# The value products of two attention pieces issued together, added up in one PSUM bank; x taken out by one ScalarE instruction a piece

## The chip, the cores and the metric

The kernel runs on one core of one Trainium2 chip. Its time is device microseconds from start to end of one execution. Each version is timed in several runs, and the median counts. The engines are named as in the profile: PE is TensorE's products, PEld its weight loads, DVE is VectorE, ACT is ScalarE, POOL is GpSimd, SP is the queue that issues nearly all transfers.

## The reference

Two layers follow each other: a local attention with a summary of the far keys, and a mixture of four experts over its output.

```python
B, H, S, D = 4, 8, 768, 64                 # attention
k_sum = k.reshape(B, H, 24, 32, D).max(axis=3)
v_sum = v.reshape(B, H, 24, 32, D).mean(axis=3)
scores_l = where(|i - j| < 16, q @ k.T / 8, -1e9)
scores_s = q @ k_sum.T / 8 + log(32)
a = softmax(concatenate([scores_l, scores_s], -1))   # sum + 1e-9
x = (a @ concatenate([v, v_sum], 2)) -> [3072, 512]

p = domain_probs / domain_probs.sum(-1)    # experts: E = 4, 512 -> 1024 -> 512
out = sum over e of p[:, e] * (relu(x @ w1[e]) @ w2[e])
```

All arrays are float32.

## The kernel before

**Pieces.** Attention is cut into 64 pieces: 4 batches, 8 blocks of 96 queries, and 2 groups of 4 heads. Piece n belongs to batch n // 16 and to group g = n % 2, so pieces n - 1 and n with n odd are the two groups of the same 96 queries. A query block needs only a window of 128 keys, and 24 summaries. Pieces 0 to 7 are made by a function of their own at the start (`first_tokens`), pieces 8 to 63 by the steps below.

**Steps of a piece.** `load_piece` fetches keys, queries and values; `stage_a` splits keys, queries and values into parts of fewer bits (the values into three bfloat16 parts, `v12` holding two and `v3` the third); `scores` forms the scores in PSUM (`psc`), takes row maxima on VectorE (`ms`, `nb`) and exponentials on ScalarE; `probs` divides by the row sum and writes the weights as float16 in `aw`: 4 heads of high parts, 4 of low parts, 4 of summaries. `transposed` turns `aw` around with one transposing transfer into `awT`. `values` multiplies: for each head, the three value parts with the weights' high part, two of them with the low part also, and the summaries `vs`. `to_x` turns what stands in PSUM into x.

**Buffers around the change.** `aw` is one of two fixed tiles: `aw1` for odd pieces below 28, `aw0` for all others, so from piece 28 on only `aw0` is used. `awT` has two buffers of its own; odd pieces below 28 take theirs from the pool of x instead. `v12` and `v3` have three buffers. PSUM has 4 banks for the experts (`ps_mm`), 2 for scores (`ps_sc`) and 2 in `ps_av`, which `px` shares with one product of the expert stage (`phd`) and with the summaries of values (`pvs`).

**Products before.** A piece has one bank, `px`. It is read as two pairs of heads (c), two columns groups (w = 0 for the products with high weights, w = 1 for those with low weights) and 96 queries. The two heads of a pair write to the lower and the upper 64 partitions, so two products with 64 weight columns each stand beside each other on the array. A product with both parts of the weights is one instruction of 192 columns; the third value part and the summaries are instructions of 96 columns. `to_x` adds the two column groups: ScalarE scales w = 1 into `xs`, VectorE adds w = 0. For pieces 8 to 15 (token block 1) ScalarE then rounds `xs` to `xh` and GpSimd subtracts to get `xl`, the two parts in which x enters the experts. From piece 16 on, `xs` is written to memory (`xd`) and read again (`xr`) when a pair of token blocks is made ready in `x_operands`.

**Order.** Token blocks of 384 rows (`TB`) are the unit of the experts: block 0, then 1, then both with the other experts, then three pairs of blocks with a seven-product scheme (`pair_units`). The expert work comes in units of a few products, and `advance` issues the attention steps between them: each step has a due time in units of pieces, and a list `ENDS` says at which due time each stage of expert work ends. From the end of the first tokens on, the instructions aren't pinned: a scheduler that replays the program on a model of the engines takes, on each engine, the ready instruction that comes first in the program, and so may put other products between the products of one piece. Transfers nearly all go through SP's queue, in the order that this scheduler gave.

The steps' due times:

```python
(k + 0.4, probs, n),
(k + 0.8, transposed, n),
(k + (1.5 if n < 2 * per else 2.0), values, n),
(k + (1.8 if n < 2 * per else 2.3), to_x, n),
```

Nearly every instruction is issued through the class `Engine`, so the profile gives all of them the line of its helper (L75). They are told apart by the names of their tiles.

Of the kernel before, what the change touches and what calls it, by code (L numbers as in the profile page):

```python
# [8 lines left out]
F32 = mybir.dt.float32  # L9
F32R = mybir.dt.float32r  # L10
BF16 = mybir.dt.bfloat16
F16 = mybir.dt.float16
AF = mybir.ActivationFunctionType
ALU = mybir.AluOpType
AX = mybir.AxisListType

P = 128
B, H, S, D = 4, 8, 768, 64
# [3 lines left out]
QB = 96  # L22
KW = 128
KA = KW + NB
NQ = S // QB
G = 4
# [4 lines left out]
NST = 5 * NB  # L31
# [14 lines left out]
ASC = 32768.0  # L46
# [16 lines left out]
def attn_moe(ctx: ExitStack, tc: tile.TileContext, qvL, qv0, v0L, kD, kT, vT, w1L, w2L, dpL, cst, out):  # L63
# [18 lines left out]
    V, A, PL, PE = (Engine(e, "rest") for e in (nc.vector, nc.scalar, nc.gpsimd, nc.tensor))  # L82
    SP = Engine(nc.sync, "load")

    def pool(name, bufs=1, **kw):
        return ctx.enter_context(tc.tile_pool(name=name, bufs=bufs, **kw))
# [3 lines left out]
    def spare_x(n):  # L90

        return n % 2 == 1 and n < XFREE

    sb = pool("sb")
    ps_mm = pool("ps_mm", 4, space=bass.MemoryType.PSUM)
    ps_sc = pool("ps_sc", 2, space=bass.MemoryType.PSUM)
    ps_av = pool("ps_av", 2, space=bass.MemoryType.PSUM)
# [21 lines left out]
    per = 2 * (TB // QB)  # L119
# [16 lines left out]
    xT = {}  # L136
    xraw = {}
    written = {}
    st = {}
# [79 lines left out]
    def stage_a(n):  # L219
        b, i, g = n // 16, (n // 2) % NQ, n % 2  # L220
        h0 = g * G
        t = st[n]
        qr = t["qv"][:, 0 : G * QB].rearrange("p (h s) -> p h s", s=QB)
        vr = t["qv"][:, G * QB :].rearrange("p (h d) -> p h d", d=D)
        kr = t["kr"]
        PL.tensor_copy(kr[:, :, KW:KA], ksum[b][:, h0 : h0 + G, :])
        ks = []
        tag, bufs = ("x", NX) if spare_x(n) else ("kl", 2)
        for half in range(2):
            k2 = sb.tile([P, 2, 2, KA], F32R, name=f"ks{n}_{half}", tag=tag, bufs=bufs)  # L230
            hs = slice(2 * half, 2 * half + 2)
            A.copy(k2[:, :, 0, :], kr[:, hs, :])
            PL.tensor_tensor(k2[:, :, 1, :], kr[:, hs, :], k2[:, :, 0, :].bitcast(F32), op=ALU.subtract)
            ks += [k2[:, 0], k2[:, 1]]
        qs = sb.tile([P, G, QB], F32R, name=f"qs{n}", tag="qs", bufs=1)
        A.copy(qs, qr)
        PL.tensor_tensor(qs[D:P], qr[D:P], qs[D:P].bitcast(F32), op=ALU.subtract)
        v12 = sb.tile([P, G, 2, D], BF16, name=f"v12_{n}", tag="v12", bufs=3)
        v3 = sb.tile([P, G, D], BF16, name=f"v3_{n}", tag="v3", bufs=3)
        A.copy(v12[:, :, 0, :], vr)  # L240
        PL.tensor_tensor(vr, vr, v12[:, :, 0, :], op=ALU.subtract)
        A.copy(v12[:, :, 1, :], vr)
        PL.tensor_tensor(v3, vr, v12[:, :, 1, :], op=ALU.subtract)
        t.update(ks=ks, qs=qs, v=(v12, v3))

    def scores(n, half):
        i = (n // 2) % NQ
        t = st[n]
        mask = masks[0 if i == 0 else (2 if i == NQ - 1 else 1)]
        if half == 0:  # L250
            t["ms"] = sb.tile([QB, G, KA], F32, name=f"ms{n}", tag="ms", bufs=2)
            t["nb"] = sb.tile([QB, G], F32, name=f"nb{n}", tag="nb", bufs=2)

            t["rs"] = sb.tile([QB, G, 2], F32, name=f"rs{n}", tag="rs", bufs=3)[:, :, 0]
        ms, nb, rs, qs, ks = (t[w] for w in ("ms", "nb", "rs", "qs", "ks"))
        heads = (2 * half, 2 * half + 1)

        def maximum(j, o, add):

            V.tensor_tensor_reduce(  # L260
                ms[:, j, :], o, add, scale=-SCALE, scalar=3.0e38,
                op0=ALU.add, op1=ALU.min, accum_out=nb[:, j : j + 1],
            )

        psc = ps_sc.tile([P, 2, 256], F32, name=f"psc{n}_{half}", tag="sc")
        for j in heads:
            o = psc[:QB, j % 2, :KA]
            PE.matmul(o, qs[:, j, :], ks[j][:, 0, :], start=True, stop=False)
            PE.matmul(o, qs[:, j, :], ks[j][:, 1, :], start=False, stop=True)
        for j in heads:  # L270
            maximum(j, psc[:QB, j % 2, :KA], mask)
        for j in heads:
            A.activation(
                ms[:, j, :], ms[:, j, :], AF.Exp, bias=nb[:, j : j + 1], scale=-1.0,
                accum_out=rs[:, j : j + 1],
            )
# [25 lines left out]
    def values(n):  # L302
        b, g = n // 16, n % 2
        t = st[n]
        awT, (v12, v3), vs = t["awT"], t["v"], vsum[b]
        px = ps_av.tile([P, 512], F32, name=f"px{n}", tag="av")
        pxv = px[:, 0 : 4 * QB].rearrange("p (c w q) -> p c w q", w=2, q=QB)
        for c in range(2):
            terms = []
            for j in (2 * c, 2 * c + 1):  # L310
                both, hi, su = awT[:, j : 2 * G : G, :], awT[:, j, :], awT[:NST, 2 * G + j, :]
                terms.append(
                    [
                        (slice(0, 2), v12[:, j, 0, :], both),
                        (slice(0, 2), v12[:, j, 1, :], both),
                        (0, v3[:, j, :], hi),
                        (0, vs[:, g * G + j, :], su),
                    ]
                )
            last = len(terms[0]) - 1  # L320
            for m in range(last + 1):
                for o in range(2):
                    w, *operands = terms[o][m]
                    PE.matmul(
                        pxv[o * D : (o + 1) * D, c, w, :], *operands, start=m == 0, stop=m == last
                    )
        t["px"] = pxv

    def x_half(name):
        return sb.tile([P, 2, TB], F32R, name=name, tag="x", bufs=NX)  # L330
# [1 line left out]
    def x_block(tb):  # L332
        return [[x_half(f"x{w}{tb}_{g}") for w in "hl"] for g in range(2)]

    def to_x(n):
        i, g = (n // 2) % NQ, n % 2
        tb, ib = n // per, i % (TB // QB)
        pxv = st.pop(n)["px"]
        xs = sb.tile([P, 2, QB], F32, name=f"xs{n}", tag="xt", bufs=2)
        A.mul(xs, pxv[:, :, 1, :], 1.0 / ASC)  # L340
        V.scalar_tensor_tensor(xs, pxv[:, :, 0, :], 1.0 / ASC, xs, op0=ALU.mult, op1=ALU.add)
        if tb < 2:
            if tb not in xT:
                xT[tb] = x_block(tb)
            xh, xl = (x[:, :, ib * QB : (ib + 1) * QB] for x in xT[tb][g])
            A.copy(xh, xs)
            PL.tensor_tensor(xl, xs, xh.bitcast(F32), op=ALU.subtract)
            return
        if (tb // 2, ib) not in xraw:
            xraw[tb // 2, ib] = dram.tile([P, 4, 2, QB], F32, name=f"xd{tb // 2}_{ib}")  # L350
        SP.dma_start(xraw[tb // 2, ib][:, 2 * g + tb % 2], xs)
        written[tb // 2, ib] = written.get((tb // 2, ib), 0) + 1

# [551 lines left out]
    steps = []  # L907
    for n in range(per, NTB * per):
        k = n + SHIFT * (n >= 2 * per)
        if n > per + 1:  # L910
            steps.append((k - 2.0, load_piece, n))
        steps += [
            (k - 0.6, stage_a, n),
            (k + 0.0, lambda m: scores(m, 0), n),
            (k + 0.3, lambda m: scores(m, 1), n),
            (k + 0.4, probs, n),
            (k + 0.8, transposed, n),
            (k + (1.5 if n < 2 * per else 2.0), values, n),
            (k + (1.8 if n < 2 * per else 2.3), to_x, n),
        ]  # L920
    for b in range(1, B):
        k = 2 * per * b + SHIFT
        steps += [(k - 2.0, setup_k, b), (k - (0.5 if b == 1 else 1.0), setup_v, b)]
# [22 lines left out]
    for (tbs, experts), end in zip(plan, ENDS):  # L946
        pair = tbs if isinstance(tbs, int) else None
        n = 2 if pair else len(tbs)
# [5 lines left out]
        parts, u, done = None, 0.0, 0.0  # L954
# [80 lines left out]
```

## Time and profile before

| | |
|---|---|
| median of 3 runs | 1190.65 us (1186.84 to 1193.61) |
| profiled execution | 1190.1 us, span 1188.3 us |
| TensorE products | 1155.9 us busy, 97% of the span |
| weight loads | 1018.8 us |
| VectorE, ScalarE, GpSimd | 640.2, 544.3, 473.2 us |
| granted TensorE clock | 0.994 |
| pieces' products (`px`) | 78.3 to 898.0 us, 896 instructions |
| memory read and written | 174.22 MB and 57.15 MB |

The span is from the first to the last instruction; the execution's time has 1.8 us more around it. Busy times of an engine count each moment once, though TensorE's products overlap: a product's length in a row is longer than the step from its start to the next one's start. What a product costs is read from the starts. After 898 us only expert work is left.

### The profile page before, as it was taken

To read this page: it belongs to the slowest core of one execution; us is meant where nothing else is said; L and a number is where in the kernel's file an instruction comes from. 1 tells how busy PE (TensorE), PEld (TensorE's weight loads), DVE (VectorE), ACT (ScalarE), POOL (GpSimd) and SP (SyncE) were. 2 spreads that over 40 slices of the span, in tenths; PEclk is the share of its full clock that TensorE was granted. 3 is DMA by queue.
4 is the path that set the end of the run, shared out by engine and by line. 5 is a ranking of instruction groups with operands and counts; after the bars stand their busy time and mean duration, and the time that the engine had idled before them with its cause. 6 is when DMAs were issued, how large, how long until landed. Compare 5 with 4: busy or idle time off the path is not lost.

```text
span 1188.3 us, 19862 instructions
## 1 busy us (share of the span) xinstructions
PE 1155.9 (97%) x6740; PEld 1018.8 (86%) x6740; DVE 640.2 (54%) x1567; ACT 544.3 (46%) x1594; POOL 473.2 (40%) x586
## 2 busy tenths in 40 slices
PE   9898899999998999999999999999999999999998
PEld 7788778888977989888898988989898998989896
DVE  6668585554797756648587543535345322323131
ACT  5577567664665746547375443535333220202020
POOL 2388686855696746546384222222203000000000
PEclk9989999999999999999999999999999999999999
DMA  6699869975986879879973758769471556556421
GB/s 238 220 283 262 241 173 270 264 198 148 319 239 193 271 236 263 245 247 289 297 240 109 211 167 268 223 195 305 115 229 42 160 176 194 179 181 201 159 98 54
DMA packets 202709, 249.60 MB, mean 210 GB/s; under 512 B 83056, under 2 KB 118896, under 8 KB 202608
## 3 DMA queue, kind: packets, MB, share of 16 engines
q1 hardware_dynamic: 202608, 248.34, 69.5%
q8 instruction: 53, 0.87, 0.3%
q14 instruction: 48, 0.39, 0.1%
HBM read 174.22 MB, written 57.15 MB: 195 GB/s over the span
## 4 chain that ended last, share of the span: by engine, by line
PE 67%; DVE 5%; DMA 2%; POOL 1%; ACT 1%; issue 1%; SPq 0%; DVEq 0%; POOLq 0%; ACTq 0%
PE po L75 37%; PE phb L75 11%; PE pha L75 7%; PE phc L75 4%; PE phd L75 4%; PE psc L75 2%; PE px L75 2%; POOL wr L75 1%; DVE xr L75 1%; DVE w1s L75 1%; DMA wr<-in_w2L 1%; PE ph L75 1%; DVE xl_t L75 1%; DVE ms L75 0%; DVE hl L75 0%
## 5 line engine op out<-in xcount | busy, mean ns | idle before, releaser
L75 PE MATMUL po<-w,hh 128*128 128x512 f32 x1536 | 482.0, 395 | 1.8 <-DVE hl L75 1.8
L75 PEld LDWEIGHTS po<-w,hh 128*128 128x128 f32 x1536 | 284.8, 189 | 63.6 <-DVE hl L75 2.3
L75 PE MATMUL po<-w,hl 128*128 128x512 f32 x768 | 303.2, 397 | 0.2 <-DVE hl L75 0.2
L75 PEld LDWEIGHTS po<-w,hl 128*128 128x128 f32 x768 | 144.7, 188 | 31.9 <-DVE hl L75 0.6
L75 POOL TENSOR_TENSOR ks<-kr,ks 128x304 fp32r<-128x304 f32 x112 | 102.1, 919 | 93.0 <-ACT ks L75 82.5
L75 PE MATMUL phb<-xh_t,w1s 128*128 128x384 f32 x384 | 114.8, 339 | 1.7 <-DVE phc L75 0.8
L75 DVE CUSTOM_DVE_ANT_0 ms<-psc,c_sb 96x152 f32<-96x152 f32 x256 | 69.0, 306 | 85.1 <-PE psc L75 82.2
L75 ACT ACTIVATE ms<-ms,nb 96x152 f32<-96x152 f32 x256 | 104.3, 415 | 19.5 <-DVE nb L75 18.6
L75 PE MATMUL pha<-xh,w 128*128 128x384 f32 x384 | 110.6, 335 | 0.0
L75 DVE SCALAR_TENSOR_TENSOR acc<-po,pw,acc 128x512 f32<-128x512 f32 x72 | 52.2, 747 | 103.9 <-PE po L75 103.9
L75 POOL TENSOR_TENSOR qv<-qv,v 128x256 f32<-128x256 f32 x56 | 42.1, 753 | 161.3 <-ACT v L75 140.0
L75 PE MATMUL ph<-xh,wh 128*128 128x384 f32 x256 | 87.7, 349 | 12.8 <-ACT wh L75 5.3
L75 PE MATMUL ph<-xh,wl 128*128 128x384 f32 x256 | 87.0, 341 | 0.4 <-POOL wl L75 0.3
L75 PE MATMUL ph<-xl,wh 128*128 128x384 f32 x256 | 86.9, 340 | 0.0
L75 ACT CAST v<-qv 128x256 bf16<-128x256 f32 x112 | 44.7, 401 | 87.5 <-PE px L75 73.4
L75 ACT CAST aw<-ms 96x512 f16<-96x512 f32 x112 | 53.4, 524 | 68.2 <-issue 49.1
L75 POOL TENSOR_TENSOR wl<-wr,wh 128x512 fp32r<-128x512 f32 x44 | 60.8, 1386 | 53.2 <-ACT wh L75 50.2
L75 DVE TENSOR_TENSOR aw<-ms,aw 96x512 f16<-96x512 f32 x112 | 71.5, 671 | 16.7 <-ACT aw L75 16.6
L75 PEld LDWEIGHTS phb<-xh_t,w1s 128*128 128x128 f32 x384 | 70.8, 188 | 4.1 <-DVE phc L75 1.7
L75 PEld LDWEIGHTS pha<-xh,w 128*128 128x128 f32 x384 | 70.5, 188 | 0.4
L75 ACT CAST ks<-kr 128x304 fp32r<-128x304 f32 x112 | 48.2, 444 | 40.3 <-PE psc L75 38.0
L75 PE MATMUL phb<-xl_t,w1s 128*128 128x384 f32 x192 | 64.3, 335 | 0.0
(123 smaller groups left out, 2190.2 us busy)
## 6 DMA issues: line engine op xcount, KB each, us to landing
w<-wd SPq DMA_DIRECT2D x80, 512.0 KB, 4.4
w1s<-wds SPq DMA_DIRECT2D x112, 256.0 KB, 3.5
w<-wd SPq DMA_DIRECT2D x84, 256.0 KB, 3.4
wr<-in_w1L SPq DMA_DIRECT2D x76, 256.0 KB, 4.3
qv<-in_qvL SPq DMA_DIRECT2D x56, 320.0 KB, 3.9
wd<-w SPq DMA_DIRECT2D x32, 512.0 KB, 4.0
wds<-w1s SPq DMA_DIRECT2D x64, 256.0 KB, 2.4
kr<-in_kD SPq DMA_DIRECT2D x56, 256.0 KB, 3.7
```

Of the source, the lines that this page charges most:

```text
L75: ins = getattr(self.engine, name)(*a, **kw)
```

## The change

`values` for an even and the odd piece after it are issued together, at the due time of the odd one (`both_values`). The two pieces share one bank, the even piece in columns 0 to 191, the odd one in 192 to 383. Each product has 96 columns, and all six of a head are added up at the same place: the column group for the low weights is gone. So a piece has 24 products of 96 columns in place of 8 of 192 and 8 of 96.

`to_x` runs once a pair. For token block 1 ScalarE scales each piece's bank half straight into `xh`, and VectorE makes `xl` from the bank and `xh`. For later pieces ScalarE scales each half into one staging tile, which holds both pieces and has one buffer (before: two of half the size), and one transfer writes it to memory. `v12` and `v3` have four buffers.

```diff
-        v12 = sb.tile([P, G, 2, D], BF16, name=f"v12_{n}", tag="v12", bufs=3)
-        v3 = sb.tile([P, G, D], BF16, name=f"v3_{n}", tag="v3", bufs=3)
+        v12 = sb.tile([P, G, 2, D], BF16, name=f"v12_{n}", tag="v12", bufs=4)
+        v3 = sb.tile([P, G, D], BF16, name=f"v3_{n}", tag="v3", bufs=4)
...
-        px = ps_av.tile([P, 512], F32, name=f"px{n}", tag="av")
-        pxv = px[:, 0 : 4 * QB].rearrange("p (c w q) -> p c w q", w=2, q=QB)
+        if g == 0:
+            t["bank"] = ps_av.tile([P, 512], F32, name=f"px{n}", tag="av")
+        else:
+            t["bank"] = st[n - 1]["bank"]
+        px = t["px"] = t["bank"][:, g * 2 * QB : (g + 1) * 2 * QB].rearrange("p (c q) -> p c q", q=QB)
...
-                both, hi, su = awT[:, j : 2 * G : G, :], awT[:, j, :], awT[:NST, 2 * G + j, :]
+                hi, lo, su = awT[:, j, :], awT[:, G + j, :], awT[:NST, 2 * G + j, :]
                 terms.append(
-                        (slice(0, 2), v12[:, j, 0, :], both),
-                        (slice(0, 2), v12[:, j, 1, :], both),
-                        (0, v3[:, j, :], hi),
-                        (0, vs[:, g * G + j, :], su),
+                        (v12[:, j, 0, :], hi),
+                        (v12[:, j, 0, :], lo),
+                        (v12[:, j, 1, :], hi),
+                        (v12[:, j, 1, :], lo),
+                        (v3[:, j, :], hi),
+                        (vs[:, g * G + j, :], su),
                 )
-            for m in range(last + 1):
+            for m in range(6):
                 for o in range(2):
-                    w, *operands = terms[o][m]
-                    PE.matmul(
-                        pxv[o * D : (o + 1) * D, c, w, :], *operands, start=m == 0, stop=m == last
-                    )
+                    PE.matmul(px[o * D : (o + 1) * D, c, :], *terms[o][m], start=m == 0, stop=m == 5)
+
+    def both_values(n):
+        values(n - 1)
+        values(n)
...
     def to_x(n):
-        pxv = st.pop(n)["px"]
-        xs = sb.tile([P, 2, QB], F32, name=f"xs{n}", tag="xt", bufs=2)
-        A.mul(xs, pxv[:, :, 1, :], 1.0 / ASC)
-        V.scalar_tensor_tensor(xs, pxv[:, :, 0, :], 1.0 / ASC, xs, op0=ALU.mult, op1=ALU.add)
+        pair = [st.pop(m)["px"] for m in (n - 1, n)]
         if tb < 2:
...
-            A.copy(xh, xs)
-            PL.tensor_tensor(xl, xs, xh.bitcast(F32), op=ALU.subtract)
+            for g in range(2):
+                A.mul(parts[g][0], pair[g], 1.0 / ASC)
+            for g in range(2):
+                V.scalar_tensor_tensor(
+                    parts[g][1], pair[g], 1.0 / ASC, parts[g][0].bitcast(F32), op0=ALU.mult, op1=ALU.subtract
+                )
             return
+        xs = sb.tile([P, 2, 2, QB], F32, name=f"xs{n}", tag="xt")
+        A.mul(xs[:, 0], pair[0], 1.0 / ASC)
+        A.mul(xs[:, 1], pair[1], 1.0 / ASC)
...
-        SP.dma_start(xraw[tb // 2, ib][:, 2 * g + tb % 2], xs)
-        written[tb // 2, ib] = written.get((tb // 2, ib), 0) + 1
+        SP.dma_start(xraw[tb // 2, ib][:, tb % 2 : 4 : 2], xs)
+        written[tb // 2, ib] = written.get((tb // 2, ib), 0) + 2
...
-            (k + (1.5 if n < 2 * per else 2.0), values, n),
-            (k + (1.8 if n < 2 * per else 2.3), to_x, n),
+        if n % 2:
+            steps += [
+                (k + (1.5 if n < 2 * per else 2.0), both_values, n),
+                (k + (1.8 if n < 2 * per else 2.3), to_x, n),
+            ]
```

More of the change, by code (lines that the diff above doesn't have):

```diff
@@ L310, in values @@
             for j in (2 * c, 2 * c + 1):
-                both, hi, su = awT[:, j : 2 * G : G, :], awT[:, j, :], awT[:NST, 2 * G + j, :]
+                hi, lo, su = awT[:, j, :], awT[:, G + j, :], awT[:NST, 2 * G + j, :]
                 terms.append(
-                    [
-                        (slice(0, 2), v12[:, j, 0, :], both),
-                        (slice(0, 2), v12[:, j, 1, :], both),
-                        (0, v3[:, j, :], hi),
-                        (0, vs[:, g * G + j, :], su),
-                    ]
-                )
-            last = len(terms[0]) - 1
-            for m in range(last + 1):
+                    (
+                        (v12[:, j, 0, :], hi),
[5 more added lines that the diff above has]
+                    )
+                )
+            for m in range(6):
                 for o in range(2):
-                    w, *operands = terms[o][m]
-                    PE.matmul(
-                        pxv[o * D : (o + 1) * D, c, w, :], *operands, start=m == 0, stop=m == last
-                    )
-        t["px"] = pxv
+                    PE.matmul(px[o * D : (o + 1) * D, c, :], *terms[o][m], start=m == 0, stop=m == 5)
+    def both_values(n):
+        values(n - 1)
+        values(n)
     def x_half(name):
@@ L335, in to_x @@
     def to_x(n):
-        i, g = (n // 2) % NQ, n % 2
+        i = (n // 2) % NQ
         tb, ib = n // per, i % (TB // QB)
-        pxv = st.pop(n)["px"]
-        xs = sb.tile([P, 2, QB], F32, name=f"xs{n}", tag="xt", bufs=2)
-        A.mul(xs, pxv[:, :, 1, :], 1.0 / ASC)
-        V.scalar_tensor_tensor(xs, pxv[:, :, 0, :], 1.0 / ASC, xs, op0=ALU.mult, op1=ALU.add)
+        pair = [st.pop(m)["px"] for m in (n - 1, n)]
         if tb < 2:
@@ L344, in to_x @@
                 xT[tb] = x_block(tb)
-            xh, xl = (x[:, :, ib * QB : (ib + 1) * QB] for x in xT[tb][g])
-            A.copy(xh, xs)
-            PL.tensor_tensor(xl, xs, xh.bitcast(F32), op=ALU.subtract)
+            parts = [[x[:, :, ib * QB : (ib + 1) * QB] for x in xT[tb][g]] for g in range(2)]
+            for g in range(2):
[3 more added lines that the diff above has]
+                    parts[g][1], pair[g], 1.0 / ASC, parts[g][0].bitcast(F32), op0=ALU.mult, op1=ALU.subtract
+                )
             return
+        xs = sb.tile([P, 2, 2, QB], F32, name=f"xs{n}", tag="xt")
+        A.mul(xs[:, 0], pair[0], 1.0 / ASC)
+        A.mul(xs[:, 1], pair[1], 1.0 / ASC)
         if (tb // 2, ib) not in xraw:
             xraw[tb // 2, ib] = dram.tile([P, 4, 2, QB], F32, name=f"xd{tb // 2}_{ib}")
-        SP.dma_start(xraw[tb // 2, ib][:, 2 * g + tb % 2], xs)
-        written[tb // 2, ib] = written.get((tb // 2, ib), 0) + 1
+        SP.dma_start(xraw[tb // 2, ib][:, tb % 2 : 4 : 2], xs)
+        written[tb // 2, ib] = written.get((tb // 2, ib), 0) + 2
     XS = ("11", "21", "22", "t1", "t2", "t3", "t4")
```

## The prediction

> **What bounds the kernel now.** I read the page's shares first, then the busy time by stretch, then TensorE's own groups, its waits, and its timeline around the changed products. The first two say whether anything off TensorE can matter.
>
> ```profile
> span 1188.3 us, 19862 instructions
> PE 1155.9 (97%) x6740; PEld 1018.8 (86%) x6740; DVE 640.2 (54%) x1567; ACT 544.3 (46%) x1594; POOL 473.2 (40%) x586
> 78.00:172.00 94.00, 83.38 (x563) 72.98 (x561) 72.35 (x172) 65.25 (x197) 74.45 (x79) 0.96 0.83 229
> 290.00:460.00 170.00, 163.61 (x1006) 143.68 (x1005) 124.70 (x282) 98.74 (x306) 115.65 (x140) 1.00 0.84 254
> 460.00:610.00 150.00, 149.02 (x864) 132.11 (x864) 99.39 (x228) 80.84 (x247) 86.42 (x108) 1.00 0.88 272
> ```
>
> Columns of the stretches: length, then busy time of PE, PEld, DVE, ACT, POOL, then clock, DMA share, GB/s. From 460 us on TensorE hardly rests (149.0 of 150 us, and so it goes on to the last products at 898), so only a change of TensorE's own work moves the end there; VectorE and ScalarE have 20 us and more to spare in each stretch. Idle TensorE time worth naming lies in 78 to 172 (10.6 us) and 290 to 460 (6.4 us). So I price TensorE's work first and the waits second.
>
> **TensorE: the products.** The groups of the value products now:
>
> ```profile
> L75 PE MATMUL px<-awT,v 128*64 128x192 f16 x448 | 36.1, 254 | 8.0 <-DMA awT<-aw 8.0
> L75 PE MATMUL px<-awT,vs 120*64 120x96 f16 x224 | 24.7, 210 | 0.0
> L75 PE MATMUL px<-awT,v 128*64 128x96 f16 x224 | 24.2, 208 | 0.0
> ```
>
> A piece has 16 of them (896 / 56): 8 of 192 columns and 8 of 96. After the change it has 24 of 96. Columns: 8 x 192 + 8 x 96 = 2304 before, 24 x 96 = 2304 after, so streaming is unchanged and only what each product and each block costs beside it counts. Busy sums don't show this, since products overlap; starts do. TensorE's timeline, one piece alone and two pieces that happen to stand together (first number the start, second the length):
>
> ```profile
> 77.78 0.40 PE L75 MATMUL po<-w,hl 128*128 128x512 f32 x1
> 78.01 0.39 PE L75 MATMUL po<-w,hh 128*128 128x512 f32 x1
> 78.33 0.40 PE L75 MATMUL px<-awT,v 128*64 128x192 f16 x6
> 78.56 0.21 PE L75 MATMUL px<-awT,vs 120*64 120x96 f16 x2
> 78.61 0.37 PE L75 MATMUL px<-awT,v 128*64 128x192 f16 x6
> 78.82 0.21 PE L75 MATMUL px<-awT,vs 120*64 120x96 f16 x2
> 78.96 0.91 PE L75 MATMUL psc<-ks,qs 128*96 128x152 f32 x8
> 79.70 0.43 PE L75 MATMUL po<-w,hh 128*128 128x512 f32 x1
> ...
> 93.46 0.33 PE L75 MATMUL ph<-xh,wl 128*128 128x384 f32 x1
> 93.64 0.34 PE L75 MATMUL ph<-xh,wh 128*128 128x384 f32 x1
> 93.91 0.40 PE L75 MATMUL px<-awT,v 128*64 128x192 f16 x6
> ...
> 94.39 0.21 PE L75 MATMUL px<-awT,vs 120*64 120x96 f16 x2
> 94.44 0.37 PE L75 MATMUL px<-awT,v 128*64 128x192 f16 x6
> ...
> 95.78 0.38 PE L75 MATMUL ph<-xl,wh 128*128 128x384 f32 x1
> ...
> 897.28 0.34 PE L75 MATMUL phd<-xh_t,w1s 128*128 128x384 f32 x1
> 897.54 0.40 PE L75 MATMUL px<-awT,v 128*64 128x192 f16 x6
> ...
> 898.17 0.73 PE L75 MATMUL po<-w,hh 128*128 128x512 f32 x2
> 898.74 0.40 PE L75 MATMUL po<-w,hl 128*128 128x512 f32 x1
> ```
>
> Inside a block the second half-piece runs from 78.61 to 78.82 plus 0.04 to 0.05 for its last pair (78.56 to 78.61): 0.25 us per half-piece, 0.50 per piece. Those 0.04 to 0.05 us are the step of one pair of 96 columns (the two products of a pair run beside each other on two halves of the array's columns), twice in a row here. Twelve such pairs make 12 x 0.043 = 0.52 us: the new form costs 0.02 us more per piece, 56 x 0.02 = **+1.1 us**.
>
> What surrounds a block is larger. The last block, one whole piece, takes 1.46 us from 897.28 to 898.74. Taken off: the phd product before it (0.18, as 93.46 to 93.64), two po products after it (0.23 each, as 77.78 to 78.01) and the piece's 0.50. That leaves 0.32 us, spread over a late first product (0.26 after its neighbour instead of 0.18), a late exit and a slow first product behind it. Is it paid by the piece or by the block? Both early blocks are followed by the same eight score products. From the last product ahead to the first behind these the single piece takes 1.69 us (78.01 to 79.70), 1.46 without its po; the two pieces take 2.14 (93.64 to 95.78), 1.96 without their ph. The second piece adds 0.50, its streaming alone. At the seam (94.39 to 94.44) nothing is lost. So the toll of about 0.3 us is paid once a block, not once a piece: that is what issuing two pieces together can save. [...]
>
> Blocks now, counted in TensorE's timeline from the first (78.33) to the last (897.54): 68. Forty-two hold one whole piece, one holds two, and 25 are fragments, because the order puts other products between the halves of some pieces. After, 28 pairs give at least 28 blocks. I don't expect 28: 12 pieces in 56 are cut now, and a pair is twice as long, so I take 12 cuts again, 40 blocks. Saved: 28 x 0.31 = **-8.7 us** (0.31, a little under the 0.32, as some of it is the slow start of what follows in any case). With no cut it is 40 x 0.31 = -12.4; with every pair cut once 12 x 0.31 = -3.7. Nearly all blocks lie where TensorE is busy without a break, so the saving is on the path.
>
> **The other engines.** What goes and what stays:
>
> ```profile
> L75 ACT ACTIVATE xs<-px 128x192 f32<-128x192 f32 x56 | 18.3, 327 | 8.4 <-PE px L75 8.4
> L75 DVE SCALAR_TENSOR_TENSOR xs<-px,xs 128x192 f32<-128x192 f32 x56 | 19.6, 349 | 8.7 <-ACT xs L75 8.5
> L75 ACT CAST xh<-xs 128x192 fp32r<-128x192 f32 x8 | 2.8, 346 | 5.6 <-DVE xs L75 5.6
> L75 POOL TENSOR_TENSOR xl<-xs,xh 128x192 fp32r<-128x192 f32 x8 | 5.6, 696 | 2.0 <-ACT xh L75 2.0
> ```
>
> The ScalarE instruction stays, 56 at 0.327. VectorE keeps 8 of 56 and loses 48 x 0.349 = 16.8 us; ScalarE loses 8 x 0.346 = 2.8 and its 5.6 us of standing behind VectorE; GpSimd loses 5.6. SP issues 24 writes to memory in place of 48, of twice the size. All of it is hidden by TensorE (VectorE is busy 124.7 of 170 us at its fullest), so I count **0**; were VectorE the bound, 16.8 us would be its worth, and that is the far end. The single staging tile is read by its write (24 of them between 172 and 898 us, one in 30 us) long before it is needed. The bank of a pair is held once instead of twice; the other user, the phd products, keeps the second one. The value tiles get a fourth buffer, and an even piece's tile still comes free by the products of the odd piece three before it, as now.
>
> **Waits.** TensorE's own, and the place at the start of the second token block (132 to 142 us):
>
> ```profile
> PE px L75 <- DMA awT<-aw: 8.0, 6, 2.6
> 132.12 0.40 PE L75 MATMUL px<-awT,v 128*64 128x192 f16 x6 [0.38 <-DMA awT<-aw]
> 137.04 1.33 PE L75 MATMUL ph<-xh,wh 128*128 128x384 f32 x4 [4.22 <-ACT xh L75]
> 136.26 0.35 DVE L75 SCALAR_TENSOR_TENSOR xs<-px,xs 128x192 f32<-128x192 f32 x1
> 138.45 0.61 PE L75 MATMUL px<-awT,v 128*64 128x192 f16 x6
> ```
>
> Piece 14's products ran at 132.12, its x waited behind VectorE until 136.26, and piece 15's products ran at 138.45. After the change both run when piece 15's transposed weights are there, so the first ph product moves from 137.04 to about 139.9 (138.45 + 1.05 of products + 0.33 of ScalarE): up to 2.9 us lost. Against it, the way from bank to x loses a VectorE step (0.35), a copy (0.35) and a GpSimd step (0.7) and ScalarE stands 5.6 us less, so piece 15 is earlier by 1 to 3 us. I take 0, with -3 and +3 as ends. The other waits for awT fall on one piece of two instead of on each; half of 8.0 is 4.0 gained if the even pieces' waits simply go, but the next paragraph takes about that back: 0.
>
> From piece 28 on all transposed weights share two buffers, and all untransposed ones a single tile:
>
> ```profile
> 310.72 2.30 SPq L75 DMA_TRANSPOSE awT<-aw  x1
> 327.06 0.40 PE L75 MATMUL px<-awT,v 128*64 128x192 f16 x6
> awT<-aw SPq DMA_TRANSPOSE x56, 4.3
> ```
>
> Piece 30 was transposed at 310.72, before piece 29's products (327.06). After, pieces 28 and 29 hold both buffers until their pair runs, so the transpose of each even piece from 30 on waits for TensorE, 17 of 36 pieces. Behind it wait the next piece's weights (the one tile is still being read) and, if the order on SP puts it ahead of a load, that load. A pair's loop is then two landings (8.6) and the making of the odd piece's weights between them, about 5 us, and 1 us of products: 15 us. By the starts of the blocks in TensorE's timeline, pairs come every 30 to 40 us after 390 us, so it is covered; between 327 and 387 us seven pieces (29 to 35) came in 60 us, 17 us a pair, so it has next to no slack there.
>
> **The sum.** -8.7 + 1.1 + 0 + 0 = -7.6 us on the profiled execution's 1190.1 (span 1188.3 and 1.8 around it): 1182.5. The median of the runs, 1190.65, stands 0.5 us above that execution, so I keep 1182.5 for both.
>
> **Rivals.** *The block is cut apart* (the change doesn't do what it says): the scheduler still fills gaps with single halves, 56 blocks: -3.7 + 1.1, 1187.5. For it: 25 fragments today; against: 42 whole pieces. *No cuts and a better start*: -12.4 + 1.1 - 3, 1176. *Weight loads set the pace.* Twelve pairs of 96 columns need a fresh set of weights each time, and 192 columns no longer cover every second load. A row with short products and heavy weights:
>
> ```profile
> 18.78 0.82 PE L75 MATMUL pav<-vf,pT 128*96 128x65 f32 x8
> 19.43 0.50 PE L75 MATMUL pT<-c_sb,ms 96*128 96x96 f32 x4
> ```
>
> Eight products of 65 columns behind 96 weight columns take 0.65 us, 0.081 each, more than their columns need. Scaled to 64 weight columns it is 0.054 a pair, 0.65 a piece instead of 0.50: 56 x 0.15 = +8.4, no gain left: 1190. Against it: two pairs in a row already step by 0.04 to 0.05. [...] *Slower: the transposes.* In that stretch, each of the four pairs leaves TensorE standing for one landing more: 4 x 4.3 = 17.2, and 1182.5 + 17 = 1199.5. It decides once the waits for awT grow by some 14 us over today's 8.0. For it: 2.6 us waits stand there already; against: TensorE has expert products to put in their place, and they are ready.
>
> **How the numbers follow.** Forecast (30 to 45 blocks, 1179 to 1186) 0.46; no cuts 0.12; cut apart 0.15; weight loads 0.09; transposes 0.18. The range reaches from below the no-cut case, 1173, to between weight loads and transposes, 1196. A change of 0.5%, 6 us, is about what can be told from none: faster is below 1184.7: 0.38 of the forecast's 0.46, 0.12 and 0.02 of the cut case, 0.52; slower above 1196.6, 0.15; within, 0.33.
>
> **What would show it.** Right: 24 products of 96 columns a piece stepping 0.042 a pair; 30 to 45 blocks; the toll still 0.3 a block; waits for awT at 5 to 11 us; VectorE near 623 us. Wrong: a step of 0.054; over 55 blocks; TensorE waits over 40 us in all, above all between 327 and 390 us or at 137 us; SP's issue of weights standing behind a transpose.

## The result, and the profile after

The changed kernel takes 1177.6 us (1174.58 to 1180.83, 6 runs) against 1189.68 in the same comparison: ratio 0.9899, 95% interval 0.9874 to 0.9924. That is 12 us faster, inside the range of the prediction (1173 to 1196) and 5 us below its 1182.5. Its profiled execution has a span of 1174.7 us, 13.5 less than before. But the steps of the forecast did not add up as forecast: the term that was to carry the gain came out at a quarter of its size, and most of the gain came from a term that had been put at zero. Ratios, here and below, leave out executions at a far lower granted clock, of which e12 had one (1603 us at 0.65).

The page's first lines, and the same stretches as before:

```profile
span 1174.7 us, 20612 instructions
PE 1150.5 (98%) x7188; PEld 1021.0 (87%) x7188; DVE 631.4 (54%) x1519; ACT 541.2 (46%) x1586; POOL 468.5 (40%) x578
78.00:172.00 94.00, 86.89 (x646) 76.58 (x645) 77.01 (x186) 65.24 (x202) 74.31 (x77) 0.98 0.92 263
290.00:460.00 170.00, 163.13 (x1105) 146.25 (x1105) 118.12 (x271) 100.92 (x311) 114.65 (x142) 0.98 0.83 252
460.00:610.00 150.00, 149.94 (x967) 133.81 (x966) 100.17 (x230) 82.58 (x254) 85.89 (x109) 1.00 0.85 268
```

Between 78 and 172 us TensorE is busy 86.9 us instead of 83.4, and the granted clock there is 0.98 instead of 0.96. From 290 to 460 nothing is better.

The value products, by group and in TensorE's timeline, one pair of pieces that was not cut:

```profile
L75 PE MATMUL px<-awT,v 128*64 128x96 f16 x1120 | 39.0, 209 | 9.4 <-DMA awT<-aw 9.4
L75 PE MATMUL px<-awT,vs 120*64 120x96 f16 x224 | 25.8, 211 | 0.1
...
199.45 0.40 PE L75 MATMUL po<-w,hl 128*128 128x512 f32 x1
199.78 0.40 PE L75 MATMUL px<-awT,v 128*64 128x96 f16 x10
200.01 0.21 PE L75 MATMUL px<-awT,vs 120*64 120x96 f16 x2
200.06 0.38 PE L75 MATMUL px<-awT,v 128*64 128x96 f16 x10
200.27 0.21 PE L75 MATMUL px<-awT,vs 120*64 120x96 f16 x2
200.32 0.38 PE L75 MATMUL px<-awT,v 128*64 128x96 f16 x10
200.53 0.21 PE L75 MATMUL px<-awT,vs 120*64 120x96 f16 x2
200.58 0.38 PE L75 MATMUL px<-awT,v 128*64 128x96 f16 x10
200.79 0.21 PE L75 MATMUL px<-awT,vs 120*64 120x96 f16 x2
200.93 0.57 PE L75 MATMUL psc<-ks,qs 128*96 128x152 f32 x4
```

From 200.06 to 200.32 six pairs of 96 columns take 0.26 us, 0.043 a pair, as priced; the seam between the two pieces (200.27 to 200.32) costs nothing. So the products are as forecast and a block still has one toll.

TensorE's largest waits, before (beside the 8.0 us for awT, shown above) and then after:

```profile
PE ph L75 <- ACT wh L75: 5.3, 4, 2.1
PE ph L75 <- ACT xh L75: 4.2, 1, 4.2
PE ph L75 <- DVE hl L75: 3.3, 4, 1.3
PE po L75 <- DVE hl L75: 1.9, 3, 1.5
```

```profile
PE px L75 <- DMA awT<-aw: 9.4, 4, 5.6
PE ph L75 <- ACT wh L75: 3.7, 2, 2.3
PE ph L75 <- DVE xl L75: 2.3, 1, 2.3
PE ph L75 <- DVE hl L75: 1.2, 1, 1.2
```

The one wait for x of block 1 fell from 4.2 to 2.3 us. The waits for `hl` (the low part of the experts' first result, made by VectorE) fell by more, from 5.2 to 1.2, and those for expert weights (`wh`) from 5.3 to 3.7.

Where the 13.5 us went, worked out from the starts in TensorE's timeline. *Edges* are the steps inside and beside blocks of value products less the usual step of each product (0.229 for po, 0.173 for 384 columns, 0.085 for scores, 0.020 for each 96 columns of a value product); *waits* are TensorE's idle times over 0.15 us, but for the 1.2 us at the very start; *slow steps* are what products away from blocks lost where each took over 0.1 us more than its usual step. In brackets is the part of the slow steps that lies in stretches of half clock; the rest came late at full clock, most of it beside a wait. The last column is when SP issued the transpose of piece 15, the last of token block 1.

| kernel | blocks | edges | waits | slow steps (at half clock) | span | piece 15 |
|---|---|---|---|---|---|---|
| before | 68 | 23.6 | 27.3 | 9.5 (4.7) | 1188.3 | 135.0 |
| changed | 57 | 21.7 | 19.1 | 5.9 (4.3) | 1174.7 | 126.4 |
| e1 fourth buffer | 66 | 23.9 | 20.9 | 10.0 (6.4) | 1184.3 | 136.1 |
| e2 sum only | 71 | 24.4 | 22.8 | 11.0 (6.8) | 1186.3 | 132.7 |
| e3 sum and buffer | 69 | 24.4 | 15.7 | 9.1 (4.7) | 1179.9 | 129.7 |
| e4 pairs and buffer | 62 | 22.4 | 23.5 | 12.6 (8.0) | 1186.6 | 131.1 |
| e5 whole blocks | 40 | 16.2 | 22.7 | 11.3 (6.6) | 1178.3 | 128.2 |
| e6 many blocks | 82 | 30.8 | 24.6 | 11.3 (7.5) | 1195.2 | 135.2 |
| e7 neutral, changed | 55 | 20.9 | 19.2 | 11.3 (7.6) | 1179.6 | 130.1 |
| e8 neutral, before | 68 | 23.9 | 24.5 | 9.9 (5.7) | 1186.7 | 136.2 |
| e9 long way in block 1 | 59 | 23.3 | 24.3 | 9.3 (7.6) | 1187.7 | 135.7 |
| e10 VectorE step back | 56 | 21.4 | 21.9 | 9.0 (5.5) | 1179.9 | 128.6 |
| e11 later in the stretch | 58 | 21.9 | 16.9 | 6.8 (3.8) | 1173.5 | 127.1 |
| e12 whole and later | 40 | 15.3 | 21.4 | 9.5 (4.6) | 1174.1 | 128.4 |

Before to changed: edges -1.9, waits -8.2, slow steps -3.6, together -13.7 of 13.5. Of the slow steps' 3.6 us only 0.4 is half clock (4.7 against 4.3).

And it happened early. At the first value product the changed trace is already 3.2 us ahead (75.1 us against 78.3), before any of the new products has run: up to there TensorE waited 2.6 us less, and between 50 and 66 us it had 3.4 us of half clock where the trace before has 6.8. This lead is not shown to come from the change: the trace of e4, which gains nothing, has it too (75.2), and that of e10, which gains 6 us, does not (78.7). The 145th po product starts at 160.8 us before and at 153.8 after (7.0 earlier), the 217th at 204.0 and 193.4 (10.6), and from there to the end the distance stays between 8.5 and 15.4.

SP's transposes, first and last of token block 1, before and then after:

```profile
68.64 2.18 SPq L75 DMA_TRANSPOSE awT<-aw  x1
...
135.00 1.33 SPq L75 DMA_TRANSPOSE awT<-aw  x1
```

```profile
66.35 1.90 SPq L75 DMA_TRANSPOSE awT<-aw  x1
...
126.44 1.31 SPq L75 DMA_TRANSPOSE awT<-aw  x1
```

Eight pieces took 66.4 us before and 60.1 after: attention itself is faster in that stretch. On TensorE none of these eight pieces stands beside its partner, though they are issued in pairs: each is a block by itself or, for piece 8, two. It is the stretch in which experts on block 0 must not run dry before x of block 1 is there.

The start of the experts on block 1, after (137.04 with a wait of 4.22 before):

```profile
129.82 0.40 PE L75 MATMUL px<-awT,v 128*64 128x96 f16 x10 [1.14 <-DMA awT<-aw]
130.46 0.74 PE L75 MATMUL psc<-ks,qs 128*96 128x152 f32 x6
131.04 0.90 PE L75 MATMUL ph<-xh,wh 128*128 128x384 f32 x4
134.24 0.44 PE L75 MATMUL ph<-xl,wh 128*128 128x384 f32 x1 [2.30 <-DVE xl L75]
```

The first ph product starts 1.2 us after piece 15's products start. It does not wait for VectorE any more; the second does, since xl is now VectorE's, behind other work in its queue (a reduction of `vch` from 132.02, row maxima from 132.89; `xl` starts at 133.83).

The slow stretch around 350 us, after:

```profile
343.69 0.40 PE L75 MATMUL px<-awT,v 128*64 128x96 f16 x10
...
349.95 0.61 PE L75 MATMUL px<-awT,v 128*64 128x96 f16 x10 [5.55 <-DMA awT<-aw]
345.00 2.82 SPq L75 DMA_TRANSPOSE awT<-aw  x1
347.00:350.00 3.00, 0.05 (x3) 0.05 (x4) 2.18 (x7) 0.92 (x4) 1.72 (x3) 0.51 0.78 125
350.00:354.00 4.00, 4.00 (x34) 3.46 (x34) 2.36 (x5) 3.04 (x10) 1.82 (x4) 0.52 0.96 286
```

Pieces 32 and 33 were issued together; 32 had its weights, 33 was transposed at 345.00, and TensorE stood 5.55 us between the two. This is the rival of the transposes, real but small: waits for awT rose from 8.0 to 9.4 us in all. The granted clock is 0.51 at the end of the wait and 0.52 in the 4 us after it.

### The profile page after: what moved, and what is told of

It is laid out like the page before. It is cut to its first block, busy times and chain, and to the rows that moved or that the text cites. A ratio compares the mean times of both kernels' runs of the same rounds, so it can differ in the third digit from the quotient of the medians.

```text
span 1174.7 us, 20612 instructions
## 1 busy us (share of the span) xinstructions
PE 1150.5 (98%) x7188; PEld 1021.0 (87%) x7188; DVE 631.4 (54%) x1519; ACT 541.2 (46%) x1586; POOL 468.5 (40%) x578
## 4 chain that ended last, share of the span: by engine, by line
PE 85%; DMA 4%; DVE 4%; POOL 3%; ACT 2%; issue 1%; SPq 1%; POOLq 0%; DVEq 0%; ACTq 0%
PE po L75 42%; PE phb L75 13%; PE pha L75 9%; PE ph L75 5%; PE phd L75 4%; PE phc L75 4%; PE psc L75 4%; PE px L75 3%; DMA vch<-in_vT 1%; PE pav L75 1%; DMA wr<-in_w2L 1%; DMA kch<-in_kT 1%; DVE ms L75 1%; SPq L75 1%; ACT ms L75 1%
## 5 line engine op out<-in xcount | busy, mean ns | idle before, releaser
L75 POOL TENSOR_TENSOR ks<-kr,ks 128x304 fp32r<-128x304 f32 x112 | 99.7, 897 | 176.8 <-ACT ks L75 160.5
L75 DVE TENSOR_TENSOR aw<-ms,aw 96x512 f16<-96x512 f32 x112 | 77.2, 723 | 21.5 <-ACT aw L75 21.3
```

The lines of the kernel that those rows point to most:

```text
L75: ins = getattr(self.engine, name)(*a, **kw)
```

## The experiments

Each was compared with runs of the kernel before on the same chip. First the parts of the change one by one: the fourth value buffer, the new products with the new way to x (*sum*), the pairing.

**e1, the fourth buffer alone.**

```diff
-        v12 = sb.tile([P, G, 2, D], BF16, name=f"v12_{n}", tag="v12", bufs=3)
-        v3 = sb.tile([P, G, D], BF16, name=f"v3_{n}", tag="v3", bufs=3)
+        v12 = sb.tile([P, G, 2, D], BF16, name=f"v12_{n}", tag="v12", bufs=4)
+        v3 = sb.tile([P, G, D], BF16, name=f"v3_{n}", tag="v3", bufs=4)
```

> The kernel before with one edit: the value tiles v12 and v3 have four buffers. Nothing else changes; 66 blocks of value products in TensorE's order (before 68, after 57). Theory 'buffer': the gain of the change came before 205 us (10.6 of 13.5 us), because ScalarE no longer stands at the value cast behind an occupied buffer (73.4 us before, 40.8 after); then this kernel alone takes 6 to 10 us, about 1181 us, and ScalarE's wait for px falls to some 40 us. Theory 'extraction' (x without the VectorE step) and theory 'pairs': no gain here, 1188 to 1191. Theory 'toll of a block': -0.6 us.

Measured: 1185.07 us, ratio 0.9967 (0.9954 to 0.998). A gain of 4 us, less than the 6 to 10 of theory "buffer", and not by its mechanism: ScalarE's wait for px at the value cast fell only from 73.4 to 68.2 us, and piece 15 was transposed at 136.1, no earlier than before. Theory "buffer" falls as the cause of the early gain.

**e2, the sum alone** (new products and new way to x, piece by piece, three buffers).

```diff
-        if g == 0:
-            t["bank"] = ps_av.tile([P, 512], F32, name=f"px{n}", tag="av")
-        else:
-            t["bank"] = st[n - 1]["bank"]
-        px = t["px"] = t["bank"][:, g * 2 * QB : (g + 1) * 2 * QB].rearrange(...)
+        bank = ps_av.tile([P, 512], F32, name=f"px{n}", tag="av")
+        px = t["px"] = bank[:, 0 : 2 * QB].rearrange("p (c q) -> p c q", q=QB)
...
+            A.mul(xh, px, 1.0 / ASC)
+            V.scalar_tensor_tensor(xl, px, 1.0 / ASC, xh.bitcast(F32), op0=ALU.mult, op1=ALU.subtract)
```

> The kernel before with the new products and the new way to x, but piece by piece: 24 products of 96 columns in a bank of its own, one ScalarE instruction, xh and xl straight from the bank, one write a piece; value tiles keep three buffers. 71 blocks. Theory 'extraction': the early gain is here, 1178 to 1183, the wait of 4.2 us at 137 us is halved. Theory 'buffer': no gain, 1188 to 1192. Theory 'weight loads' (now unlikely): +8. Theory 'toll': 71 blocks instead of 68, +0.9, and +1.1 for the products, 1191.

Measured: 1188.13 us, ratio 0.9993 (0.9979 to 1.0007): no change. Piece 15 came 2.3 us earlier, but TensorE waited 4.3 us for xl at 143. The short way alone brings no gain either.

**e3, the sum and the fourth buffer** (the change without its pairing).

> The same as the sum alone, with four buffers for the value tiles: the change without its pairing. 69 blocks. If the pairing is worth nothing, this equals the changed kernel, 1177.6. Theory 'toll': the changed kernel has 12 blocks fewer, so this one is 3.7 us slower than it, 1181. Theory 'pairs' (the early gain comes from issuing two pieces together): 1188.

Measured: 1181.76 us, ratio 0.995 (0.9932 to 0.9968). Piece 15 at 129.7, TensorE's waits 15.7 us, the least of all. So sum and buffer together are worth 6 us, half of the gain. The edges are as before (24.4 us for 69 blocks).

**e4, pairs and the fourth buffer** with the old products and the old way to x.

```diff
+        if n % 2:
+            steps += [
+                (k + (1.5 if n < 2 * per else 2.0), both_values, n),
+                (k + (1.8 if n < 2 * per else 2.3), both_to_x, n),
+            ]
```

> The kernel before with pairs issued together and four buffers, but the old products (8 of 192 and 8 of 96 columns, two column groups, a bank a piece) and the old way to x, both pieces at the odd piece's due time. 62 blocks. Theory 'extraction': no gain, 1187 to 1190. Theory 'buffer': 1180 to 1183. Theory 'toll': 6 blocks fewer, -1.9 on top of what the buffer gives. (Pairs with three buffers can't be ordered at all: the third odd tile would wait for products that come after it.)

Measured: 1189.38 us, ratio 1.0001 (0.9986 to 1.0016). Pairing with the old way to x gives nothing that can be measured: in its profile fewer blocks bring 1.2 us at the edges and the waits 3.8, slow steps, all of it half clock, take 3.1 back, and the median does not move.

Then the toll of a block, at 40 and at 82 blocks with the same products.

**e5, whole blocks.**

```diff
-                    PE.matmul(px[o * D : (o + 1) * D, c, :], *terms[o][m], start=m == 0, stop=m == 5)
+                    tc.keep_in_program_order(
+                        nc.tensor.matmul(px[o * D : (o + 1) * D, c, :], *terms[o][m], start=m == 0, stop=m == 5)
+                    )
```

> The changed kernel, each value product kept behind the TensorE instruction issued before it in the program: 40 blocks instead of 57, the same products. Theory 'toll' (0.31 us a block): the time at the edges of blocks falls from 21.7 to some 16.5 us, and the kernel takes 5 us less, 1172. Theory 'order' (the edges are cover for waits that appear elsewhere): the edges fall and TensorE's waits rise by as much, 1176 to 1180.

Measured: 1178.91 us, ratio 0.9912 (0.9888 to 0.9936), no different from the changed kernel. The edges fell as priced, from 21.7 to 16.2 us for 17 blocks fewer: 0.33 a block. Waits (+3.6) and slow steps (+5.4, of which 2.3 are half clock) took it back, some of it at a place where the changed kernel has none:

```profile
460.00:610.00 150.00, 146.89 (x913) 131.68 (x913) 96.77 (x219) 78.28 (x238) 82.58 (x106) 0.99 0.87 267
591.39 0.69 PE L75 MATMUL phb<-xh_t,w1s 128*128 128x384 f32 x1 [1.75 <-DVE phc L75]
```

Of the 460 to 610 stretch TensorE is busy 146.9 us, not 149.9. Theory "toll" has the right price, theory "order" the right outcome.

**e6, many blocks.**

```diff
     def both_values(n):
-        values(n - 1)
-        values(n)
+        with tc.high_priority(offset=RUSH):
+            values(n - 1)
+            values(n)
```

> The changed kernel with a raised priority for the value products: TensorE's order has 82 blocks instead of 57, 29 of them a single product. Theory 'toll': +25 blocks x 0.31 = +7.8 us at the edges, 1185. A single product as a block may cost less than a whole toll; then +4 to +6, 1182. Theory 'order': the products come as early as they can, waits fall, and the kernel stays near 1178.

Measured: 1201.23 us, ratio 1.0106 (1.0077 to 1.0134), 24 us slower than the changed kernel. The edges rose by 9.1 us for 25 blocks, 0.36 each. A single product costs a whole toll:

```profile
841.10 0.23 PE L75 MATMUL px<-awT,v 128*64 128x96 f16 x1
841.26 0.51 PE L75 MATMUL po<-w,hl 128*128 128x512 f32 x1
841.70 0.23 PE L75 MATMUL px<-awT,v 128*64 128x96 f16 x1
```

One value product and one po product take 0.60 us from start to start, against 0.23 and 0.02: 0.35 of toll. In the profiled execution, 20.5 us longer than the changed kernel's, the rest is waits (+5.5) and slow steps (+5.4, of which 3.2 are half clock); block 1 was slow again (piece 15 at 135.2). No theory named this time ahead: the toll accounts for less than half of it, and why the waits rose is open.

Next, what the draw of the scheduler's order is worth by itself.

**e7 and e8, a neutral edit in the changed kernel and in the one before.**

```diff
-SHIFT = 1.12
+SHIFT = 1.10
```

> The changed kernel with the due times of pieces from 16 on earlier by 0.02 of a piece (SHIFT 1.10 instead of 1.12), an edit that means nothing by itself but lets the scheduler draw another order; 55 blocks. If what the order draws is worth little, 1176 to 1179; if it is worth as much as the early gain, anything from 1170 to 1186.

> The kernel before with the same neutral edit (SHIFT 1.10); 68 blocks. If what the order draws is worth little, 1188 to 1191; if much, 1182 to 1198.

Measured: the changed kernel 1181.92 us, ratio 0.9933 (0.9909 to 0.9958); the kernel before 1187.89, ratio 0.9994 (0.9979 to 1.0009). In the profile of e7 edges and waits are those of the changed kernel (20.9 and 19.2) and the slow steps are 11.3 instead of 5.9 (at half clock 7.6 instead of 4.3). The interval of e7 still overlaps that of the changed kernel (0.9874 to 0.9924), and e8 moved by 1 us. So a difference of up to 4 us between two versions of this kernel can be the draw; two neutral edits are few to bound it by. The 12 us of the change and the 24 of e6 are well beyond it; e1's 4 and the distance from e3 to the changed kernel can be the draw.

Last, which part of the way to x matters, and whether the stall at 350 us can go.

**e9, the long way for block 1 only.**

```diff
-            for g in range(2):
-                A.mul(parts[g][0], pair[g], 1.0 / ASC)
-            for g in range(2):
-                V.scalar_tensor_tensor(
-                    parts[g][1], pair[g], 1.0 / ASC, parts[g][0].bitcast(F32), op0=ALU.mult, op1=ALU.subtract
-                )
+            for g in range(2):
+                V.tensor_scalar_mul(xs[:, g], pair[g], 1.0 / ASC)
+                A.copy(parts[g][0], xs[:, g])
+                PL.tensor_tensor(parts[g][1], xs[:, g], parts[g][0].bitcast(F32), op=ALU.subtract)
```

> The changed kernel, but x of token block 1 (pieces 8 to 15) goes the long way again: VectorE scales the bank into a staging tile, ScalarE rounds it to xh, GpSimd subtracts to xl. Everything else as changed. 59 blocks. Theory 'extraction': the short way to xh is what cut the wait of the first experts' products on block 1 (4.2 us at 137 before, 2.3 at 134 after); then the waits between 78 and 172 us rise from 6.9 to 9 us or more and the time to about 1181. Theory 'pairs and buffer': no change beyond the draw of the order, 1176 to 1181.

Measured: 1186.43 us, ratio 0.9974 (0.9962 to 0.9987): 9 us of the change's 12 are gone, with eight pieces of 56 edited. The transposes and the stretch:

```profile
135.74 1.71 SPq L75 DMA_TRANSPOSE awT<-aw  x1
78.00:172.00 94.00, 81.43 (x585) 71.97 (x585) 75.04 (x174) 63.59 (x189) 77.01 (x82) 0.91 0.86 239
```

Piece 15 is back at 135.7, TensorE is busy 81.4 us of 94, and the clock is 0.91. The loss is complete by 167 us: the 145th po product comes 13.1 us later than in the changed kernel, and stays about there. This execution is the slowest of twelve, 3 us over their median, and 2.8 of the 13.1 us are there at the first value product (77.9 us), before any x is taken out. The median's 9 us is twice the distance that e7 calls the draw, and most of the loss lies in the stretch named ahead. So, as far as one order of each can show, most of the gain needs the new way to x in block 1, together with the pairing and the buffer.

The mechanism of theory "extraction" is not what e9 shows, though. It said that the first experts' products on block 1 would wait longer for x; here they do not wait for x at all. Between 133 and 146 us TensorE stands for keys of the next scores (1.9 us, ScalarE's ks), for piece 15's weights (3.4) and for summaries (1.6, ScalarE's vs): the attention steps are late. Why the long way delays them is not shown. Nor is it the old way step for step: VectorE scales into the one staging tile, which the changed kernel does not use for block 1.

**e10, the VectorE step back** for pieces 16 to 63.

```diff
-        A.mul(xs[:, 0], pair[0], 1.0 / ASC)
-        A.mul(xs[:, 1], pair[1], 1.0 / ASC)
+        for g in range(2):
+            A.mul(xs[:, g], pair[g], 1.0 / ASC)
+            V.scalar_tensor_tensor(xs[:, g], pair[g], 0.0, xs[:, g], op0=ALU.mult, op1=ALU.add)
```

> The changed kernel with a VectorE instruction a piece put back for pieces 16 to 63 (bank times zero plus the staged value, in place; 48 x 0.35 = 16.8 us of VectorE, one more step before the write). 56 blocks. The prediction's 0 for the other engines says 1176 to 1181; were the VectorE step worth its length, 1194; if its place in the queues matters (SP stood 64.5 us behind this step before), 1181 to 1185.

Measured: 1181.83 us, ratio 0.995 (0.9938 to 0.9961). That is 4 us more than the changed kernel and as much as the neutral edit gives, so it can't be told from the draw. Its length, 16.8 us, is not what it costs; whether 0 or 4 stays open.

**e11, products later between pieces 28 and 35.**

```diff
-                (k + (1.5 if n < 2 * per else 2.0), both_values, n),
-                (k + (1.8 if n < 2 * per else 2.3), to_x, n),
+                (k + (1.5 if n < 2 * per else 2.5 if 28 <= n < 36 else 2.0), both_values, n),
+                (k + (1.8 if n < 2 * per else 2.8 if 28 <= n < 36 else 2.3), to_x, n),
```

> The changed kernel with the products of pieces 28 to 35 due half a piece later (2.5 instead of 2.0, x at 2.8). The two waits for transposed weights at 333 and 350 us (1.3 and 5.6 us, the larger followed by 6.8 us of half clock) should go: TensorE has other products at that place. Theory 'transposes': -5 to -8, 1170 to 1173. If the whole loop of the two awT buffers moves later with the products, the wait stays: 1176 to 1181.

Measured: 1175.67 us, ratio 0.9892 (0.988 to 0.9905). TensorE's waits:

```profile
PE px L75 <- DMA awT<-aw: 4.5, 3, 1.8
PE psc L75 <- POOL qs L75: 4.0, 2, 2.3
```

The wait for awT at 350 is gone (9.4 to 4.5 in all), and two waits of score products for GpSimd stand in the same stretch, at 347 and 362 us. This speaks for a stretch bound by its attention steps and not by one transfer; the gain of 2 us is within the draw.

**e12, both.**

> Both: 40 whole blocks and the later due times for pieces 28 to 35. If toll and waits add up, 5 us less at the edges than the changed kernel and the waits at 335 and 352 us (2.0 and 3.9 there) gone: 1170 to 1174, the fastest of all. If waits take the place of what the edges give, as with whole blocks alone, 1177 to 1180.

Measured: 1177.21 us, ratio 0.9893 (0.9877 to 0.991). Edges 15.3, waits 21.4, slow steps 9.5: again what the edges gave (6.4) went to waits and slow steps (5.9), with waits for `qs` again in the stretch of pieces 28 to 35 (at 348 and 363 us). No version here is faster than the changed kernel beyond the draw.

## Why the prediction was right, and where it was wrong

The time was right, for reasons that were mostly not the ones given: one term fell short by 5.7 us and another, put at zero, gave more than that. That they met inside the range is luck. The forecast's own case, 30 to 45 blocks and 1179 to 1186 us, did not come: there were 57 blocks and 1177.6 us, and "over 55 blocks" was one of its signs of being wrong.

- *The products, +1.1.* Right: pairs of 96 columns step by 0.043 us, also twelve and more in a row. The rival of the weight loads (0.054) is out.
- *The toll, 0.31 a block, paid once a block.* Right: 0.33 by e5, 0.36 by e6, and a lone product costs all of it. What causes it at the edges and not at the seam is not shown.
- *The number of blocks, 40.* This is the step that failed. There are 57, 11 fewer than before and not 28. Only 12 of the 28 pairs stayed whole, 9 blocks are one piece by itself and the rest are fragments. I had carried over the cuts of single pieces; but a pair is also cut where TensorE can begin the even piece while the odd one's weights are not there (pieces 8 and 9 begin at 75.1 and 82.8 us), as in all four pairs of block 1. The counts that the expectations of the experiments name ahead came out in the traces, so this number could have been counted before the run. With the products' +1.1 in them the edges gave 1.9 us, not 7.6. The rival "cut apart" (56 blocks) described what happened, and its time of 1187.5 would have been the forecast of these terms.
- *The waits, 0.* Wrong, and it made up for the other. TensorE's waits fell by 8.2 us. The prediction saw both sides at the start of block 1: up to 2.9 lost by holding back the even piece, and 1 to 3 us gained by the shorter way from bank to x. The loss did not come: the pieces of block 1 ran one by one, piece 14 at 127.1 us, before piece 15's weights were there (129.8). The shorter way it priced at one place, the end of block 1, where the wait for x gave 1.9 of the 8.2. In the trace all eight pieces went faster: 66.4 us from first to last transpose became 60.1. The new way with no pairing took 63.4 (e2), pairing and buffer with the old way 63.7 (e4), and e9 65.4; e6, with the new way and its products issued early, took 67.5. So the new way, and the pairing with the buffer, seem worth about 3 us each there, on one trace each, and the order of the products matters as well. Which of the three queues that the long way passes slowed the pieces was not separated. Of the 8.2 us, 2.6 fell before the first value product, where the change is not shown to be the cause, and 3.7 from there to 172 us.
- *The half clock.* Not in the sum at all. Products away from blocks lost 4.7 us to it before and 4.3 after, so it hardly bears on the gain; over the fourteen traces it lies between 3.8 and 8.0. The other 3.2 us of slow steps came at full clock, most of it beside waits.
- *The transposes.* The rival was right in its place (between 327 and 387 us) and far too dear: 1.4 us of waits more, not 17. Only one pair stood long, 5.55 us, and up to 2 us of half clock behind it (half of the 3.9 us from 349.95 to 353.86) come on top. In the other pairs TensorE did have expert products to put there.
- *The other engines, 0.* Not contradicted, and not shown: e10 lies at the draw's edge. VectorE's busy time fell by 8.8 us, to 631.4, and not by 16.8 to 623: making the weights (`aw` and `rs`) took 9 us longer in all.

## What to carry to other kernels

In this kernel the value products cost a toll of 0.33 to 0.36 us (e5, e6) for each block in which they stand between other products, so count blocks in the order that is really issued and not in the program. Where one stage feeds the next through several engines, price a shorter way on the pace of the whole stage and not at its last step only. And measure what a neutral edit does under a scheduler that draws its own order: here 1 and 4 us, so a single difference of that size between two versions is not evidence.

## What the hardware showed that was not expected

After waits TensorE's granted clock is 0.5 for 3.4 or 6.8 us in these traces, in e6 and e9 once for 10.2. Before, around the wait of 4.2 us at 137 us:

```profile
132.00:137.00 5.00, 0.70 (x16) 0.56 (x16) 4.32 (x8) 1.82 (x7) 1.24 (x4) 1.00 0.68 181
137.00:141.00 4.00, 3.96 (x26) 3.52 (x27) 0.83 (x1) 2.01 (x6) 4.00 (x6) 0.57 0.86 242
```

Here the clock is 1.00 while TensorE stands and 0.57 when it works again, so the wait of 4.2 us cost up to another 1.7 behind it (half of the 3.41 us from 137.45 to 140.87; products of 384 columns step by 0.320 us there and by 0.173 at a clock of 1.00). The half clock can also begin within the wait, as at 347 us after.

The length of one wait does not decide. Waits of 1.4 us (e11, at 130 us) and 1.75 us (e5, at 591 us) came with half clock; waits of 2.6 us (before, at 360 us) and 2.95 us (e12, at 348 us) did not. Within a trace the half clock starts whole multiples of 3.413 us apart: in the changed kernel at 50.07, 135.40 and 347.03 us, 25 and 62 times that length, and it lasts 3.41, 3.41 and 6.83 us there. Cut into such stretches from 45 us on, the fourteen traces show half clock after each of the 39 stretches in which TensorE, at full clock, stood idle 55% of the time or more, after none of the 4414 with less than 30%, and after 14 of the 69 between. So in these traces what a wait cost went with the whole idle share of the stretch in which it fell, and not with its length alone. What sets the stretches and the clock behind them is not shown.
